# RWKV-6 followed by a SiLU feed-forward layer: four sums of weight slices moved to an earlier stage and another engine, one load moved to another buffer slot, a scaling moved to ScalarE

## The chip, the cores and the metric

The kernel runs on one core of a Trainium2 chip. The metric is the device time of one execution in microseconds (us); before the change it is 572.14 us, the median of 3 runs (571.52 to 572.37). Engines are called as in the profile: PE (TensorE), DVE (VectorE), ACT (ScalarE), POOL (GpSimd), SP (SyncE, which here only issues transfers).

## The reference

```python
# r, k, v, w: (4 batches, 8 heads, 768 tokens, 48), float32;  u: (8, 48)
for t in range(S):
    cur = u * k_t outer v_t
    y[:, :, t] = r_t @ (state + cur)
    state = w_t[:, None] * state + k_t outer v_t
x = y as (4 * 768 tokens, 8 * 48 = 384)
h = x @ w_in                 # 384 x 2048, given as float64
out = (h * sigmoid(h)) @ w_out   # 2048 x 384, given as float64
```

## The kernel before, in words

**Units.** The 768 tokens are cut into 6 stretches of 128, the 4 batches into 2 pairs. A unit is one stretch of one pair, so there are 12 units, numbered 0 to 11 here as in the code (the change's "fourth unit" is unit 3). Every unit passes three phases, and phases of different units run beside each other: attention of unit i, the first layer ("ups") of unit i-1, the second layer ("downs") of unit i-2.

**Attention of a unit.** r, k and w come in token order into `raw`, a buffer with two slots and rooms for w, r and k in each. Unit i uses slot i % 2 up to unit 3 and slot 0 from unit 4 on (`slot`, L98). DVE transposes the rooms into `tw`, `tr`, `tk` (`turn`, L361). The 128 x 128 score matrix is built in 7 levels: at each, POOL multiplies keys by products of decays (`start_keys` L666, `grow_own` L651, `grow_keys` L642; the products themselves are L410), DVE does so with the queries (`grow_queries` L624, `prepare` L779), PE multiplies them (L700), and the result is kept in `score` by DVE (`keep_masked`, L718) or ACT (`keep_level`, L800). Two levels go to PE together, in a "burst" at levels 1, 3 and 5. The diagonal, the bonus with u, is summed apart: up to unit 3 by `bonus` (POOL, L436 to L440), `bonus_sum` (DVE, L445 and L449, then four small transfers), `bonus_spread` (ACT copies L588 and L590, a DVE shuffle L591) and `bonus_write` (DVE, L598, one for each half e of the heads); from unit 4 on in blocks of 8 tokens by `block_bonus` (POOL, L493), `block_sum` (DVE, L530), transfers through DRAM, `block_turn` (L563) and `block_write` (L569). Then `y_state` (PE, L843 and L850) and `y_values` (PE L864, ACT copies L869) make y, and `update` makes the new state: PE products (L909), the old state scaled by the decay, and DVE's sum of both (L932). The scaling is done by POOL for units 2 and 3 (L914, two multiplications) and by ACT from unit 4 on (L927, eight activations of 48 columns).

**The weights** arrive as float64. Sixteen pieces (eight of w_in, eight of w_out) are rounded to float32 by ACT (L228, L230, L236), DVE (L247, L248) and POOL (L260), up to about 99 us.

**The feed-forward layers.** From unit 1 on the second layer is a product of 2 x 2 blocks done with seven multiplications (`quarter`, L1329; "quarter 6" is the last of them), on sums of activations (`sums`, DVE, L1300) and on four sums of w_out blocks (`weight_sums`, DVE, L1285). A quarter's result leaves PSUM by L1334 (ACT) or L1337 (DVE). From unit 3 on (`NFAST`) the first layer is done with 20 multiplications on sums of slices of x (`sums_of_x`, DVE) and of w_in (`in_weight_sum`, L1124): 21 additions of 128 x 512, named m, n, q14, q3 and so on in `weight_plan`. Their results stand in eight rooms: two in `in_sum`, six in slot 1 of `raw` (two each in its w, r and k rooms), or in place in `w_in_sb`. Their first reader is unit 3's first layer (L1185), which starts at 190.79 us in the profile.

**Order of the work.** Each engine runs its queue in the order in which the Python code issues it (no scheduler). The first three units are written out by hand in `do(...)` lists at the end; from unit 3 on `mix(i)` gives a list of groups, and after each group a number of steps of the downs and ups is issued. The loop that calls `mix` appends the weight sums to groups by number: six names for DVE (m in group 4, n in 5, m1 and m2 in 6, q12a and q12 in 8; `weight_sums(3)` second in group 4), the rest on POOL (q14 and q3 in group 7, q, n13 and t in 10, u1, u and q19 in 11; the last seven names, in the next unit, are left where they are).

Of the kernel before, what the change touches and what calls it, by code (L numbers as in the profile page):

```python
# [38 lines left out]
def kernel(  # L39
# [11 lines left out]
    nc = tc.nc  # L51
# [4 lines left out]
    NL = 7  # L56
    NB = 2
# [9 lines left out]
    NSLOT = 2  # L67
    NTOK = 2
    NPAIR = 4
# [28 lines left out]

    def slot(i, name):

        return 0 if i >= NPAIR else i % NSLOT

    def twos(room):

# [354 lines left out]
    at = 768  # L459
# [441 lines left out]
    def update(i, b):  # L901
        n, b0 = units[i]
        if n == S // L - 1:
            return
        if b == 0:
            p_kv[i] = bank("p_m" if i < NTOK else "p_sc", NB, NP, D)
        for p in range(NP):
            for e in range(2):
                nc.tensor.matmul(p_kv[i][PD * e:PD * e + D, b, p, :], lhsT=kq[i, b][:, p, PD * e:PD * e + D],  # L909
                                 rhs=values(i, b)[:, 2 * p + e, :], start=(b == 0 and p == 0),  # L910
                                 stop=(b == NB - 1 and p == NP - 1))
        new = state[:, b0 + b]
        if n > 0 and i < NPAIR:
            nc.gpsimd.tensor_tensor(out=new, in0=new,  # L914
                                    in1=tw[i][NL][:, b * NP:(b + 1) * NP, :].to_broadcast([128, NP, D]),
                                    op=ALU.mult)
        if b == NB - 1 and i < NPAIR:
            add_update(i)

    def add_update(i):  # L920
        n, b0 = units[i]
        if n == S // L - 1:
            return
        for b in range(NB if i >= NPAIR else 0):
# [30 lines left out]
    def both(fn, i, *args):  # L955
        return [(fn, i, b, *args) for b in range(NB)]
# [4 lines left out]
    def mix(i):  # L961

        ahead = i + 1 < len(units)

        def at(now, *steps):
            return steps if now else ()

        def bonus_steps(j, *steps):
            return [(block_bonus, j, x) for x in steps]

        def sum_steps(j, *steps):
            return [(block_sum, j, x) for x in steps]
# [7 lines left out]
        def products_of(j, *ls):  # L980
            return [(product, j, l) for l in ls]

        end = [[*at(ahead, *bonus_steps(i + 1, 0, 1, 2, 3))],
               [*at(i < len(units) - NB, (turn_apart, i), (turn_k, i)), (y_state, i), *both(y_values, i), *at(ahead, *turns(i + 1)), *at(ahead and i > NFAST, *sum_steps(i + 1, 0, 1)),
                *at(i <= NFAST, (sums, i - 1, FH // 2 - 2)), *both(update, i), *at(not ahead, (move_x, i))]]
        if i < NPAIR:
# [5 lines left out]
                      [(prepare, i, 3), (reverse_v, i), (bonus, i, 0), (bonus_sum, i, 0)],  # L992
                      [(bonus, i, 1), (burst, i, 3), (keep_level, i, 3), (bonus, i, 2)],
                      [(keep_level, i, 4), (go_on, i, 4), (bonus_sum, i, 1), (load_rk, i + 1), (load_u,)],
                      [(prepare, i, 5), (make_block_mask,), (bonus_spread, i)],
                      [(burst, i, 5), (keep_level, i, 5, 0), (keep_level, i, 6, 0), (go_on, i, 6), *at(i == NPAIR - 1, *both(turn, i + 1, "w")), (bonus_write, i, (0,)), (keep_level, i, 5, 1), (keep_level, i, 6, 1), (bonus_write, i, (1,))], *end]
            groups = list(zip(groups, (1, 1, 0, 2, 1, 1, 1, 1, 1, 2, 2, 1, 1)))
        else:
            j = i - 1
# [21 lines left out]
            else:  # L1021
# [3 lines left out]
                def loads(name, *gs):  # L1025
# [18 lines left out]
                          ([(burst, i, 5), (keep_level, i, 5, 0), (keep_level, i, 6, 0), *at(ahead, *bonus_steps(i + 1, 0)), (go_on, i, 6), (block_turn, i), *at(i > NPAIR + 1, (block_write, i, 1))], 2),  # L1044
# [319 lines left out]
    def do(*steps):  # L1364
        for fn, *args in steps:
            fn(*args)
# [39 lines left out]
    for m in range(1, 4):  # L1406
# [4 lines left out]
    do((scores, 1, NL - 1), (bonus, 2, 0), (bonus, 2, 1), (join_weight, 8), (add_weight,), (bonus_sum, 2, 0), (bonus, 2, 2), (up, 0, 7), (turn_apart, 1), *both(x_products, 1),  # L1411
       (turn_k, 1), *both(x_copy, 1), (tail_weight, 9), (head_weight, 9),
       (join_weight, 9), (add_weight,), *both(update, 1), (up, 1, 0), (tail_weight, 10), (head_weight, 10), (bonus_sum, 2, 1), *both(turn, 2, "w"))
# [22 lines left out]
    for i in range(3, len(units)):  # L1436
        steps = downs(i - 2) + ups(i - 1)
        groups = mix(i)
        if i == NTOK + 1:
            groups[4][0].insert(1, (weight_sums, 3))  # L1440
            for place, engine, names in ((4, nc.vector, ("m",)), (5, nc.vector, ("n",)), (6, nc.vector, ("m1", "m2")), (7, nc.gpsimd, ("q14", "q3")),
                                         (8, nc.vector, ("q12a", "q12")), (10, nc.gpsimd, ("q", "n13", "t")), (11, nc.gpsimd, ("u1", "u", "q19"))):
                groups[place][0].append((in_weight_sum, engine, *names))
        if i == NFAST + 1:
            keep_banks()
            for place, engine, names in ((5, nc.gpsimd, ("q7",)),
                                         (8, nc.gpsimd, ("q8", "q1")), (9, nc.gpsimd, ("q5", "q9")), (14, nc.gpsimd, ("q6", "q17"))):
# [40 lines left out]
```

## Time and profile before

| | |
|---|---|
| time, median of 3 runs | 572.14 us (571.52 to 572.37) |
| the profiled execution's own time | 571.82 us |
| its span (first to last instruction) | 570.0 us |
| PE busy / weight loads | 556.4 us / 517.9 us |
| DVE / POOL / ACT busy | 477.6 / 396.8 / 270.6 us |
| granted TensorE clock | 0.997 of full speed |

The page of the profile gives busy time by engine, then the queues and the chain of work that ended last. The view of waits lists, for each engine, what ended its idle time. The timeline gives runs of equal instructions in order of time: start, duration from the first to the end of the last, engine, line, operation, tile written and tiles read, shapes, count, and in brackets the idle time ahead and what ended it.

### The profile page before, as it was taken

The numbers are of one execution on the slowest core, as the hardware profiler recorded it, in microseconds if no ns is written. First come the engines' busy times: TensorE is split into PE (matmuls) and PEld (weight loads), VectorE is DVE, ScalarE is ACT, GpSimd is POOL, SyncE is SP. The second block draws the span as 40 slices with busy tenths as digits, with TensorE's granted clock in tenths as the row PEclk, the third lists the DMA queues.
The fourth block names the chain that finished last, engine by engine and source line by source line (L and its number), as shares of the span: only waits on it lengthen the run. The fifth ranks groups of instructions, "written<-read, shape, count | busy, mean of one in ns | idle before, by whom it ended". The sixth has DMA issues, their size and how long they took to land.

```text
span 570.0 us, 18875 instructions
## 1 busy us (share of the span) xinstructions
PE 556.4 (98%) x7782; PEld 517.9 (91%) x7782; DVE 477.6 (84%) x745; ACT 270.6 (47%) x604; POOL 396.8 (70%) x450
## 2 busy tenths in 40 slices
PE   8989999999998999899999999999999999999997
PEld 7768776698888999899999999999999999999997
DVE  7979798898999899879989989989989989882250
ACT  5779695442451373273274274274274272371330
POOL 6998868637999998795696696696696696700000
PEclk9989999999999999999999999999999999999999
DMA  9957776444255365265464465365465462102000
GB/s 224 316 114 204 183 230 113 49 84 101 74 90 100 69 112 94 58 130 93 73 129 89 87 120 94 71 128 94 93 106 96 91 109 65 37 6 56 29 9 21
DMA packets 206485, 57.59 MB, mean 101 GB/s; under 512 B 186048, under 2 KB 198208, under 8 KB 206400
## 3 DMA queue, kind: packets, MB, share of 16 engines
q1 hardware_dynamic: 203712, 54.23, 46.3%
q10 hardware_dynamic: 2688, 2.16, 1.6%
q8 instruction: 61, 1.00, 0.8%
q14 instruction: 24, 0.20, 0.1%
HBM read 47.14 MB, written 9.18 MB: 99 GB/s over the span
## 4 chain that ended last, share of the span: by engine, by line
PE 76%; DVE 9%; POOL 8%; issue 2%; DMA 2%; ACT 1%; SPq 1%; DVEq 0%; POOLq 0%
PE p_o L1329 24%; PE p_o L1185 15%; PE p_h L1185 10%; PE p_h L1078 6%; PE p_h L1329 4%; PE p_m L1267 4%; POOL tk L642 2%; PE p_sc L700 2%; PE p_m L864 2%; DVE temps L1300 2%; PE p_sc L1329 2%; DVE score L718 2%; PE p_m L843 1%; PE p_m L700 1%; DMA raw<-in_r_dram 1%
## 5 line engine op out<-in xcount | busy, mean ns | idle before, releaser
L642 POOL TENSOR_TENSOR tk<-tk,tw 128x256 f32<-128x256 f32 x112 | 93.2, 853 | 7.1 <-DVE tw L410 3.1
L1329 PE MATMUL p_o<-own,temps 128*128 128x192 f32 x496 | 82.9, 326 | 1.5 <-DVE temps L1300 1.5
L1329 PEld LDWEIGHTS p_o<-own,temps 128*128 128x128 f32 x496 | 80.8, 190 | 1.8 <-DVE temps L1300 1.8
L1185 PE MATMUL p_o<-xt,w_in_sb 128*64 128x128 f32 x1152 | 72.1, 273 | 0.6 <-POOL w_in_sb L1124 0.6
L1078 PE MATMUL p_h<-xt,w_in_sb 128*128 128x256 f32 x288 | 67.7, 391 | 0.8 <-POOL w_in_sb L260 0.8
L1185 PEld LDWEIGHTS p_o<-xt,w_in_sb 128*64 128x64 f32 x1152 | 64.7, 137 | 0.8 <-POOL w_in_sb L1124 0.8
L1078 PEld LDWEIGHTS p_h<-xt,w_in_sb 128*128 128x128 f32 x288 | 54.7, 194 | 9.4 <-POOL w_in_sb L260 1.1
L410 POOL TENSOR_TENSOR tw<-tw 128x256 f32<-128x256 f32 (+6 forms) x71 | 38.8, 546 | 33.0 <-DVE tw L361 29.6
L1329 PE MATMUL p_o<-w_out_sb,gt 128*128 128x192 f32 x308 | 54.4, 329 | 1.4 <-DVE ob L1337 1.4
L493 POOL TENSOR_TENSOR ruk<-tokens_rk 128x384 f32<-128x384 f32 x48 | 54.3, 1151 | 0.0
L1329 PEld LDWEIGHTS p_o<-w_out_sb,gt 128*128 128x128 f32 x308 | 50.1, 190 | 2.3 <-DVE ob L1337 1.7
L624 DVE TENSOR_TENSOR tr<-tr,tw 128x512 f32<-128x512 f32 x57 | 51.1, 896 | 0.6
L651 POOL TENSOR_TENSOR tk<-tk,tw 128x256 f32<-128x256 f32 x32 | 24.8, 806 | 30.7 <-DVE tk L361 30.7
L1300 DVE TENSOR_TENSOR temps<-gt 128x512 f32<-128x512 f32 (+1 forms) x48 | 44.6, 965 | 0.0
L1334 ACT COPY partial<-p_o 128x192 f32<-128x192 f32 x31 | 9.9, 319 | 70.5 <-PE p_o L1329 70.5
L612 ACT COPY tk<-tk 128x256 f32<-128x256 f32 x52 | 21.0, 403 | 38.0 <-POOL tk L642 29.0
L1209 ACT ACTIVATE gt<-p_o 128x512 f32<-128x512 f32 x45 | 26.1, 601 | 25.6 <-PE p_o L1185 25.6
L718 DVE COPY_PREDICATED score<-mask,p_sc 128x512 f32<-128x512 int8 x42 | 31.2, 798 | 0.8 <-PE p_sc L700 0.6
L1329 PE MATMUL p_o<-w_out_sb,temps 128*128 128x192 f32 x176 | 30.4, 326 | 0.0
L493 POOL TENSOR_TENSOR spare<-tokens_rk 128x384 f32<-128x384 f32 x24 | 29.1, 1228 | 0.6
L1329 PE MATMUL p_h<-w_out_sb,gt 128*128 128x192 f32 x168 | 29.1, 326 | 0.0
L1329 PEld LDWEIGHTS p_o<-w_out_sb,temps 128*128 128x128 f32 x176 | 28.9, 190 | 0.0
(252 smaller groups left out, 1308.0 us busy)
## 6 DMA issues: line engine op xcount, KB each, us to landing
w_out_sb<-in_moe_w_in_dram SPq DMA_DIRECT2D x6, 768.0 KB, 6.9
turned<-yt SPq DMA_DIRECT2D x18, 192.0 KB, 2.7
xt<-turned SPq DMA_DIRECT2D x9, 384.0 KB, 3.3
w_out_sb<-in_moe_w_out_dram SPq DMA_DIRECT2D x4, 768.0 KB, 5.1
own<-in_moe_w_out_dram SPq DMA_DIRECT2D x4, 768.0 KB, 6.5
tokens_w<-in_w_dram SPq DMA_DIRECT2D x8, 384.0 KB, 4.4
tokens_rk<-in_r_dram SPq DMA_DIRECT2D x7, 384.0 KB, 4.7
tokens_rk<-in_k_dram SPq DMA_DIRECT2D x7, 384.0 KB, 5.7
```

The source lines that it names most:

```text
L410: engine.tensor_tensor(out=up, in0=t[:, :, 0::2], in1=t[:, :, 1::2], op=ALU.mult)
L493: mul = lambda out, one, two: nc.gpsimd.tensor_tensor(out=out, in0=one, in1=two, op=ALU.mult)
L624: nc.vector.tensor_tensor(out=odd, in0=odd, in1=tw[i][l][:, :, 0::2][:, :, :, None].to_broadcast([128, Q, L >> (l + 1), c]), op=ALU.mult)
L642: nc.gpsimd.tensor_tensor(out=out, in0=have, in1=odd_products(i, l, b, *blocks), op=ALU.mult)
L651: nc.gpsimd.tensor_tensor(out=have, in0=have, in1=odd_products(i, l, b, [2, NP * ni]), op=ALU.mult)
L718: nc.vector.copy_predicated(out=dst, mask=masks[l][:, :, None].to_broadcast([128, NB, NP, ni, c]), data=sc[e].rearrange("p (b q) (i c) -> ...
L1078: nc.tensor.matmul(p_h[:, a, :], lhsT=w_in_sb[:, c, f * 128:(f + 1) * 128], rhs=xt[i][:, c, :], start=(a == 0 and c == 0), stop=(a == 1 an ...
L1185: nc.tensor.matmul(p[h:h + PD, q, :], lhsT=left[:, f:f + PD], rhs=right, start=first and q == 0, stop=q == 3, skip_group_check=True)
L1209: nc.scalar.activation(out=g(f, t), in_=have, func=AF.Silu)
L1267: nc.tensor.matmul(po[i, b], lhsT=gt[i, f // 2][:, f % 2, b * L:(b + 1) * L], rhs=w_out_sb[:, f, :], start=(f == 0), stop=(f == FC - 1))
L1300: nc.vector.tensor_tensor(out=out, in0=one, in1=two, op=op)
L1329: nc.tensor.matmul(p, lhsT=left(f), rhs=right[:, f, :], start=which in (0, 1, 3) and f == 0, stop=f == FH - 1, skip_group_check=True)
```

## The change

In words, by its parts:

- Unit 3's r is loaded into slot 0 of `raw` and not slot 1, so the r room of slot 1 is free from unit 1 on. The eight rooms are dealt out anew: m and t in `in_sum`, n and n13 in slot 1's w room, q14 and q3 in its r room, m1 and q12 in its k room.
- m, q14, q3 and q are summed on POOL in the hand-written list of the rounding: m and q14 behind `bonus(2, 2)`, q3 and q behind piece 9's addition. Before, m was DVE's and the others POOL's, all in unit 3.
- The other sums of unit 3: n goes from group 5 to 7, m1 and m2 from 6 to 8, q12a and q12 from 8 to 9 (all DVE), n13 and t from 10 to 9 (POOL). `weight_sums(3)` goes from the second to the last place of group 4.
- The state's scaling in units 2 and 3 goes from POOL (L914) to ACT (L927).
- Unit 3's `bonus_spread` goes from group 9 to 10, behind the first half's `keep_level`.
- In unit 5, `block_sum` 3 goes behind `keep_level(i, 3)`, and `block_write(i, 1)` goes two groups earlier, as in units 6 to 11.

```diff
     def slot(i, name):
-        return 0 if i >= NPAIR else i % NSLOT
+        return 0 if i >= NPAIR or (i, name) == (NPAIR - 1, "r") else i % NSLOT
...
-        if n > 0 and i < NPAIR:
+        if n > 0 and i < NTOK:
             nc.gpsimd.tensor_tensor(out=new, in0=new,
...
-        for b in range(NB if i >= NPAIR else 0):
+        for b in range(NB if i >= NTOK and n > 0 else 0):
...
-                      [(prepare, i, 5), (make_block_mask,), (bonus_spread, i)],
-                      [(burst, i, 5), ..., *both(turn, i + 1, "w")), (bonus_write, i, (0,)), ...
+                      [(prepare, i, 5), (make_block_mask,)],
+                      [(burst, i, 5), ..., *both(turn, i + 1, "w")), (bonus_spread, i), (bonus_write, i, (0,)), ...
...
-                          ([(burst, i, 3), *sum_steps(i, 3), (keep_level, i, 3), *sum_steps(i, 4)], 2),
+                          ([(burst, i, 3), *at(i > NPAIR + 1, *sum_steps(i, 3)), (keep_level, i, 3), *at(i == NPAIR + 1, *sum_steps(i, 3)), *sum_steps(i, 4)], 2),
...
-                          ([..., (block_turn, i), *at(i > NPAIR + 1, (block_write, i, 1))], 2),
+                          ([..., (block_turn, i), (block_write, i, 1)], 2),
                           ([(keep_level, i, 5, 1), (keep_level, i, 6, 1)], 1),
-                          ([*at(i == NPAIR + 1, (block_write, i, 1)), (block_write, i, 0)], 1),
+                          ([(block_write, i, 0)], 1),
...
-        e = dict(zip(("m", "n", "t", "n13", "m1", "q12", "q14", "q3"), rooms))
+        e = dict(zip(("m", "t", "n", "n13", "q14", "q3", "m1", "q12"), rooms))
...
-    do(..., (bonus, 2, 2), (up, 0, 7), ...
+    do(..., (bonus, 2, 2), (in_weight_sum, nc.gpsimd, "m", "q14"), (up, 0, 7), ...
-       (join_weight, 9), (add_weight,), *both(update, 1), ...
+       (join_weight, 9), (add_weight,), (in_weight_sum, nc.gpsimd, "q3", "q"), *both(update, 1), ...
...
-            groups[4][0].insert(1, (weight_sums, 3))
-            for place, engine, names in ((4, nc.vector, ("m",)), (5, nc.vector, ("n",)), (6, nc.vector, ("m1", "m2")), (7, nc.gpsimd, ("q14", "q3")),
-                                         (8, nc.vector, ("q12a", "q12")), (10, nc.gpsimd, ("q", "n13", "t")), (11, nc.gpsimd, ("u1", "u", "q19"))):
+            groups[4][0].append((weight_sums, 3))
+            for place, engine, names in ((7, nc.vector, ("n",)), (8, nc.vector, ("m1", "m2",)), (9, nc.vector, ("q12a", "q12",)), (9, nc.gpsimd, ("n13", "t",)), (11, nc.gpsimd, ("u1", "u", "q19",)),):
                 groups[place][0].append((in_weight_sum, engine, *names))
```

More of the change, by code (lines that the diff above doesn't have):

```diff
@@ L994, in mix @@
                       [(keep_level, i, 4), (go_on, i, 4), (bonus_sum, i, 1), (load_rk, i + 1), (load_u,)],
-                      [(prepare, i, 5), (make_block_mask,), (bonus_spread, i)],
-                      [(burst, i, 5), (keep_level, i, 5, 0), (keep_level, i, 6, 0), (go_on, i, 6), *at(i == NPAIR - 1, *both(turn, i + 1, "w")), (bonus_write, i, (0,)), (keep_level, i, 5, 1), (keep_level, i, 6, 1), (bonus_write, i, (1,))], *end]
+                      [(prepare, i, 5), (make_block_mask,)],
+                      [(burst, i, 5), (keep_level, i, 5, 0), (keep_level, i, 6, 0), (go_on, i, 6), *at(i == NPAIR - 1, *both(turn, i + 1, "w")), (bonus_spread, i), (bonus_write, i, (0,)), (keep_level, i, 5, 1), (keep_level, i, 6, 1), (bonus_write, i, (1,))], *end]
             groups = list(zip(groups, (1, 1, 0, 2, 1, 1, 1, 1, 1, 2, 2, 1, 1)))
@@ L1043, in mix @@
                           ([*loads("r", 3)], 1),
-                          ([(burst, i, 5), (keep_level, i, 5, 0), (keep_level, i, 6, 0), *at(ahead, *bonus_steps(i + 1, 0)), (go_on, i, 6), (block_turn, i), *at(i > NPAIR + 1, (block_write, i, 1))], 2),
+                          ([(burst, i, 5), (keep_level, i, 5, 0), (keep_level, i, 6, 0), *at(ahead, *bonus_steps(i + 1, 0)), (go_on, i, 6), (block_turn, i), (block_write, i, 1)], 2),
                           ([(keep_level, i, 5, 1), (keep_level, i, 6, 1)], 1),
-                          ([*at(i == NPAIR + 1, (block_write, i, 1)), (block_write, i, 0)], 1),
+                          ([(block_write, i, 0)], 1),
                           ([*at(ahead, *bonus_steps(i + 1, 1, 2, 3)), ], 2),
@@ L1409 @@
        (bonus_write, 1))
-    do((scores, 1, NL - 1), (bonus, 2, 0), (bonus, 2, 1), (join_weight, 8), (add_weight,), (bonus_sum, 2, 0), (bonus, 2, 2), (up, 0, 7), (turn_apart, 1), *both(x_products, 1),
+    do((scores, 1, NL - 1), (bonus, 2, 0), (bonus, 2, 1), (join_weight, 8), (add_weight,), (bonus_sum, 2, 0), (bonus, 2, 2), (in_weight_sum, nc.gpsimd, "m", "q14"), (up, 0, 7), (turn_apart, 1), *both(x_products, 1),
        (turn_k, 1), *both(x_copy, 1), (tail_weight, 9), (head_weight, 9),
-       (join_weight, 9), (add_weight,), *both(update, 1), (up, 1, 0), (tail_weight, 10), (head_weight, 10), (bonus_sum, 2, 1), *both(turn, 2, "w"))
+       (join_weight, 9), (add_weight,), (in_weight_sum, nc.gpsimd, "q3", "q"), *both(update, 1), (up, 1, 0), (tail_weight, 10), (head_weight, 10), (bonus_sum, 2, 1), *both(turn, 2, "w"))
     blocks = block_loads(3)
@@ L1445 @@
             keep_banks()
-            for place, engine, names in ((5, nc.gpsimd, ("q7",)),
-                                         (8, nc.gpsimd, ("q8", "q1")), (9, nc.gpsimd, ("q5", "q9")), (14, nc.gpsimd, ("q6", "q17"))):
+            for place, engine, names in ((5, nc.gpsimd, ("q7",)), (8, nc.gpsimd, ("q8", "q1",)), (9, nc.gpsimd, ("q5", "q9",)), (14, nc.gpsimd, ("q6", "q17",)),):
                 groups[place][0].append((in_weight_sum, engine, *names))
```

## The prediction, as put on record before the changed kernel ran

> **What bounds the kernel.** I read the busy shares first, then who PE waited for, then the timelines of PE, DVE and POOL around each of those waits. The first page gives (busy us, share, instructions):
>
> ```profile
> PE 556.4 (98%) x7782; PEld 517.9 (91%) x7782; DVE 477.6 (84%) x745; ACT 270.6 (47%) x604; POOL 396.8 (70%) x450
> ```
>
> PE is the bound. The change leaves PE's instructions as they are, so it can only give what PE idles. The waits (total us, times, longest) are few:
>
> ```profile
> PE p_sc L700 <- POOL tk L666: 1.5, 1, 1.5
> PE p_o L1329 <- DVE temps L1300: 1.5, 1, 1.5
> PE p_o L1329 <- DVE ob L1337: 1.4, 1, 1.4
> PE p_m L1372 <- POOL ident masks.py:199: 1.4, 1, 1.4
> PE p_m L700 <- POOL tk L642: 1.3, 2, 1.0
> PE p_m L850 <- DMA raw<-in_r_dram: 0.9, 1, 0.9
> ...
> PE p_o L1185 <- POOL w_in_sb L1124: 0.6, 1, 0.6
> ```
>
> PE's timeline places them. The first and the fourth lie ahead of 40 us, where nothing changes. Six lie in the changed stretch: 1.03 us at 133.56 (unit 3's first burst), 1.47 at 178.45, 0.56 at 202.05, 1.38 at 231.77, 0.23 at 249.33, 0.88 at 257.97. They add up to **5.55 us**, the most that can be won. After 258 us PE never waits, so what is won there stays won.
>
> Behind these waits two engines are full. The table by stretches (us, then PE, weight loads, DVE, ACT, POOL) shows DVE and POOL both over 92% busy:
>
> ```profile
> 135.00:178.50 43.50, 42.03 (x442) 38.15 (x440) 41.36 (x55) 14.94 (x38) 40.03 (x40) 1.00 0.46 90
> ```
>
> And they slow each other. The same DVE addition of 128 x 256 takes 0.41 us while POOL idles (103.06) and 1.22 us beside POOL; two equal POOL multiplications take 1.47 us together at 92.20, and 2.94 us at 130.57 beside a DVE subtraction of 1.74 us:
>
> ```profile
> 103.06 0.41 DVE L1300 TENSOR_TENSOR temps<-temps,gt 128x256 f32<-128x256 f32 x1
> 163.70 1.22 DVE L1300 TENSOR_TENSOR temps<-temps,gt 128x256 f32<-128x256 f32 x1
> 92.20 1.47 POOL L642 TENSOR_TENSOR tk<-tk,tw 128x256 f32<-128x256 f32 x2 [0.39 <-ACT tk L612]
> 130.57 2.94 POOL L642 TENSOR_TENSOR tk<-tk,tw 128x256 f32<-128x256 f32 x2 [0.57 <-ACT tk L612]
> 130.46 1.74 DVE L1285 TENSOR_TENSOR w_out_sb<-w_out_sb,own 128x1536 f32<-128x1536 f32 x1
> ```
>
> **Part by part.**
>
> *Four sums into the rounding.* POOL idles there twice:
>
> ```profile
> 73.10 1.83 POOL L260 TENSOR_TENSOR w_out_sb<-temps 128x768 uint32<-128x768 uint32 x1 [2.44 <-DMA raw<-in_r_dram]
> 78.36 1.82 POOL L260 TENSOR_TENSOR w_out_sb<-temps 128x768 uint32<-128x768 uint32 x1 [3.43 <-ACT temps L228]
> ```
>
> L1124 on POOL costs 1.27 us undisturbed (155.03; 193.84), two of them 2.55, in gaps of 2.44 and 3.43. DVE does roundings, PSUM copies and transposes meanwhile, which keep their length beside POOL (L247 0.96 at 71.01 with POOL idle, 0.93 at 79.37 beside L260). The first gap overflows by 0.1 us. The additions' reader is PE's second layer: piece 11's L260 ends at 83.65, and its blocks f = 6, 7 come in the later half of PE's L1267 group at 83.66, so about 1.3 us of slack. At the slowest L1124 on POOL (2.30 at 158.07) the four would take 9.2 us, 3.3 more than the gaps, and PE would lose 2.0. I take 0, since the undisturbed row fits. The sums read only w_in, rounded by 63 us, and slot 1's r room was last read for unit 1; unit 3's r goes to slot 0 at 104.9, after unit 2's r was transposed (81.28 to 82.6); unit 4's r is issued at 156.69, after unit 3's transpose at 127.4. So the moved load waits for nothing and stays in its place in SP's queue.
>
> What it removes later: on DVE m (0.73); on POOL q14 and q3 (2.95 at 147.02) and q (1.27).
>
> *Scaling on ACT.* Removed from POOL: 2.04 us at 118.97 and 1.34 at 173.26. Added to ACT: eight activations, 1.91 us at 217.64. In unit 2 they stand behind the copies of y (L869, 119.97 to 122.34), so they end at 124.25, and DVE's L932 starts at 124.3 and not 123.47: **+0.85 us** for DVE's queue, whose next are unit 3's transposes, for which POOL (L410, L666, L642) and then the burst at 133.56 wait. In unit 3 they end at 170.0, long before L932 (175.79), and push one L1087 and the issue of x_out by 0.15 us; sums_of_x reads that x only at 184.53, so nothing.
>
> *`weight_sums(3)` behind the masked copies.* The 1.74 us subtraction no longer stands beside L642: that pair goes from 2.94 to 1.47. With +0.85 the keys are ready at 133.56 + 0.85 - 1.47 = 132.95 against PE's 132.53: the wait falls from 1.03 to 0.4 (between 0 and 1.9, if nothing is relieved). The subtraction now ends about 137.0; quarter 6 reads its result at 139.49, or 138.9 with PE earlier: covered by 1.9.
>
> *Wait at 178.45.* DVE has hardly any idle time from 137 to 178, so its own gain decides. It loses m (0.73) and n's 1.48 goes to a place where DVE would wait for the burst at 142.18; `bonus_sum` then comes about 1 us earlier, and POOL, without q14 and q3, does level 4's keys at 147.1 and not 149.97. I put the end of `bonus_write` at 160.6, before it is 161.43: 0.85. It can't be much earlier, since ACT copies both_b 1.04 us later than before, behind the first four-and-two L800: at about 156.8, and the second L800 end at 158.6. Then come 16 sums (L1300). POOL's bonus of unit 4, held behind q, n13 and t until 160.32 so far, starts when its r and k have landed, about 156.4, and is through with u1, u, q19 and L410 at 169.4; the last of the first eight sums runs free, which gives 0.4 more. DVE's gain is 1.25; with a little for L914 gone, **1.5 us**, which is PE's whole gain up to here (0.6 at 133 is inside it). Bounds: 0, if POOL's removed work is filled by the work behind it; 2.1 (1.47 + 0.6), the whole wait.
>
> The Trainium skill, "SBUF — State Buffer", section "Who interferes with whom", states that a DVE instruction with two SBUF inputs and a GpSimd one that reads SBUF exclude each other for a whole instruction. The rows above agree (the pair is longer by 1.47 beside 1.74). If that were the entire account, the POOL work taken out before 178 in unit 3 (2.95 + 1.27 + 1.34) would come off DVE's queue whole and the wait would be gone, a sum better by 0.6. My sum stays with the queue as walked through.
>
> *Wait at 202.05* is for q9. POOL does q7, q8 and q1 before level 4's L642 (197.68), whose ACT copy is ready at 197.19. With POOL earlier, that copy, which follows PE, becomes the gate: 0.49 earlier. **0.5** (0 to 0.56).
>
> *Wait at 231.77.* DVE's queue stands 0.89 us behind POOL's L493, which follows the DVE transposes of unit 5, slowed by POOL before. Relative to PE, POOL is earlier by that same 0.5 only: **0.5** (0 to 1.38). At 249.33: 0.1 (0 to 0.23).
>
> *Unit 5's order.* The releaser named at 257.97 is a transfer long done; DVE's row shows the real one:
>
> ```profile
> 254.30 3.61 DVE L569 COPY_PREDICATED score<-spare 128x1024 f32<-128x1024 int8 x2 [0.72 <-ACT score L800]
> 257.81 2.09 DVE L1300 TENSOR_TENSOR temps<-gt 128x512 f32<-128x512 f32 x2
> ```
>
> The second of two L569 ends at 257.8. Now one runs at 251.1 (DVE is idle 1.77 us there, and block_both has landed, as the shuffle at 250.89 shows) and the other ends near 255.4, against PE's 257.09: **0.88** (0.5 to 0.88). `block_sum` 3 behind `keep_level` moves DVE's work between two waits for POOL: 0.
>
> **Sum:** 1.5 + 0.5 + 0.5 + 0.1 + 0.88 = 3.5 us off 571.82, the profiled execution (span 570.0 and 1.8 around it): 568.3. The median of the runs is 0.3 higher, so **568.6 us**.
>
> **Rivals.**
>
> - *All six waits go.* POOL's earlier sums free both queues enough. For it: both are over 92% full. Against it: after 195 us POOL's gates are ACT copies that follow PE. 572.14 - 5.55 = 566.6.
> - *DVE stays as late at 178.* The freed POOL time is filled at once by unit 4's bonus, which then disturbs the same DVE sums. Only 0.5 and 0.88 remain: 570.8.
> - *It doesn't do what it says:* PE's waits reappear at the next instruction, as its chain alternates between DVE and POOL. Against it: after 258 us nothing waits. 572.1.
> - *Slower: the late sums hold up DVE.* n, m1, m2, q12a and q12 now run beside level 4's and 5's L642 and n13, t; they took 6.2 us (0.68 to 2.18 each). At 2.18 each they take 10.9: 4.7 more, less 0.73 for m and 1.4 won elsewhere, is +2.6: 574.7. It decides from 9.5 us for the five. Against it: POOL has less to do there now.
>
> **Chances.** Forecast 0.50, all waits gone 0.14, DVE as late 0.13, nothing 0.12, slower 0.11. The case of 570.8 is split by the bound of 0.2% (1.14 us, about what a measurement here can tell from no change: below 571.0 is faster): 0.09 faster, 0.04 same. Faster 0.73, same 0.16, slower 0.11. The range takes in all waits gone and no change: 566.3 to 572.3.
>
> **What would show it.** Right: L1124 on POOL between 70 and 78 us with L260 at its old times; L642 after the first transposes of unit 3 at about 1.5 us a pair and PE's wait there under 0.6; the wait before L1329 near 177 under 0.7; L569's second end before PE's L850 in unit 5. Wrong: a new PE wait between 78 and 130 (rounding held up), L932 at 125 or later, or DVE's L1124 of over 1.9 us each.

## The result, and the profile after

The changed kernel takes **570.47 us** (median of 8 runs, 569.81 to 571.70), the kernel before in the same comparison 572.23 us (8 runs): a ratio of 0.9973, 95% interval 0.9962 to 0.9984. The gain is 1.76 us, half of the 3.5 forecast. The profiled execution was one of the slower ones of the changed kernel (571.49 us, span 569.7), and so was the one in a second profile of it, from run e1 below (571.38 us, where the median is 570.16), which stands beside it in what follows.

The first page of the changed kernel (busy us, share, instructions) and its view of waits for PE (total, times, longest):

```profile
PE 555.2 (97%) x7782; PEld 516.5 (91%) x7782; DVE 476.4 (84%) x744; ACT 274.6 (48%) x620; POOL 394.5 (69%) x447
```

```profile
PE p_o L1329 <- DVE temps L1300: 1.6, 1, 1.6
...
PE p_o L1329 <- DVE ob L1337: 1.2, 1, 1.2
PE p_m L1267 <- POOL w_out_sb L260: 0.9, 1, 0.9
...
PE p_m L700 <- POOL tk L642: 0.6, 2, 0.4
PE p_o L1185 <- POOL w_in_sb L1124: 0.3, 1, 0.3
```

The largest wait in the changed stretch, for DVE's L1300, has not shrunk. A new one has come (L1267, for a rounding). The one for POOL's L642 is down from 1.0 to 0.4, and that for L569 in unit 5 is gone.

PE does the same 7782 matmuls in the same order in both, so the time between two fixed PE instructions compares the kernels stretch by stretch, whatever came before. In us:

| from, to (start in the profile before) | before | after | e1 | e10 |
|---|---|---|---|---|
| rounding: L1267 (78.33) to L1267 (92.17) | 13.84 | 15.16 | 14.34 | 13.84 |
| unit 3's first burst, first product to second (133.56) | 1.73 | 1.06 | 1.06 | 1.06 |
| unit 3's L843 (163.52) to unit 4's third burst (189.70) | 26.18 | 26.31 | 26.45 | 24.57 |
| to unit 4's L843 (211.06) | 21.36 | 21.32 | 21.14 | 21.87 |
| to unit 5's third burst (234.56) | 23.50 | 23.29 | 23.48 | 22.86 |
| unit 5's L843 (255.96) to L909 (259.79) | 3.83 | 2.64 | 2.65 | 2.64 |

The other stretches of these profiles are alike to 0.3 us; the work before 66 us, which the change doesn't touch, ends between 0.2 us earlier and 0.9 us later than in the profile before (in e1 0.9, in e5 3.3).

**Rounding.** POOL's timeline (start, us from the first to the end of the last, instruction, count, and in brackets the idle time ahead) in the changed kernel:

```profile
67.59 0.99 POOL L436 TENSOR_TENSOR spare<-tokens_rk 128x384 f32<-128x384 f32 x1 [4.51 <-DMA tokens_rk<-in_k_dram]
...
75.11 1.29 POOL L1124 TENSOR_TENSOR raw<-w_in_sb 128x512 f32<-128x512 f32 x1
76.34 1.84 POOL L260 TENSOR_TENSOR w_out_sb<-temps 128x768 uint32<-128x768 uint32 x1
...
80.61 1.85 POOL L260 TENSOR_TENSOR w_out_sb<-temps 128x768 uint32<-128x768 uint32 x1
```

The four sums cost what was forecast, 1.3 us each. But unit 2's r and k landed 3.3 us later than in the profile before (L436 at 67.59, there 64.32), and with the gaps filled POOL can't catch up: L260 stands at 76.34 and 80.61, before at 73.10 and 78.36, and PE waits 0.92 us for it at 85.99.

**The sums of unit 3 (L1300), for which PE waits near 178 us.** DVE's timeline of the changed kernel, from the end of `bonus_write` on:

```profile
162.34 2.36 DVE L1300 TENSOR_TENSOR temps<-gt 128x256 f32<-128x256 f32 x2
164.62 1.23 DVE L1300 TENSOR_TENSOR temps<-temps,gt 128x256 f32<-128x256 f32 x1
165.89 1.38 DVE L1300 TENSOR_TENSOR temps<-gt,temps 128x256 f32<-128x256 f32 x1
167.19 2.91 DVE L1300 TENSOR_TENSOR temps<-gt 128x256 f32<-128x256 f32 x2
170.02 1.26 DVE L1300 TENSOR_TENSOR temps<-temps,gt 128x256 f32<-128x256 f32 x1
171.31 0.42 DVE L1300 TENSOR_TENSOR temps<-gt,temps 128x256 f32<-128x256 f32 x1
172.14 1.30 DVE L361 STREAM_TRANSPOSE tk<-raw 128x512 f32<-128x512 f32 x2 [0.40 <-DMA raw<-in_w_dram]
...
177.40 1.82 DVE L1300 TENSOR_TENSOR temps<-gt 128x256 f32<-128x256 f32 x2
179.15 0.41 DVE L1300 TENSOR_TENSOR temps<-temps,gt 128x256 f32<-128x256 f32 x1
```

and POOL's beside them:

```profile
159.29 3.97 POOL L493 TENSOR_TENSOR ruk<-ruk,u_bc 128x384 f32<-128x384 f32 x2
...
165.53 1.46 POOL L1124 TENSOR_TENSOR w_in_sb<-w_in_sb 128x512 f32<-128x512 f32 x1
167.06 1.33 POOL L1124 TENSOR_TENSOR w_in_sb<-raw,w_in_sb 128x512 f32<-128x512 f32 x1
168.48 1.34 POOL L1124 TENSOR_TENSOR w_in_sb<-w_in_sb 128x512 f32<-128x512 f32 x1
...
177.33 1.61 POOL L651 TENSOR_TENSOR tk<-tk,tw 128x256 f32<-128x256 f32 x2
```

POOL's bonus of unit 4 (L493) and u1, u, q19 (the three L1124) start 2.5 to 3 us earlier than before, and the first eight sums still stand beside them: they take 9.39 us to the end of the eighth (171.73), before 9.75. Late in the queue the second pair of L651 now falls beside the last four sums: the pair of sums at 177.40 takes 1.82, before it took 1.03. PE starts when the fifteenth sum ends, at 179.56. The rows of the profile before, DVE's and then POOL's:

```profile
169.80 1.38 DVE L1300 TENSOR_TENSOR temps<-gt,temps 128x256 f32<-128x256 f32 x1
...
176.94 1.03 DVE L1300 TENSOR_TENSOR temps<-gt 128x256 f32<-128x256 f32 x2
```

```profile
179.17 1.44 POOL L651 TENSOR_TENSOR tk<-tk,tw 128x256 f32<-128x256 f32 x2
```

### The profile page after: what moved, and what is told of

It is laid out like the page before. It is cut to its first block, busy times and chain, and to the rows that moved or that the text cites. A ratio compares the mean times of both kernels' runs of the same rounds, so it can differ in the third digit from the quotient of the medians.

```text
span 569.7 us, 18886 instructions
## 1 busy us (share of the span) xinstructions
PE 555.2 (97%) x7782; PEld 516.5 (91%) x7782; DVE 476.4 (84%) x744; ACT 274.6 (48%) x620; POOL 394.5 (69%) x447
## 4 chain that ended last, share of the span: by engine, by line
PE 70%; DVE 11%; POOL 8%; DMA 3%; ACT 3%; SPq 2%; issue 2%; DVEq 0%; POOLq 0%; ACTq 0%
PE p_o L1329 24%; PE p_o L1185 14%; PE p_h L1185 9%; PE p_h L1329 4%; PE p_m L1267 3%; PE p_h L1078 2%; PE p_sc L700 2%; PE p_m L864 2%; POOL tk L642 2%; DVE temps L1300 2%; PE p_sc L1329 2%; DVE score L718 2%; DMA raw<-in_k_dram 2%; PE p_m L843 1%; PE p_m L700 1%
## 5 line engine op out<-in xcount | busy, mean ns | idle before, releaser
L642 POOL TENSOR_TENSOR tk<-tk,tw 128x256 f32<-128x256 f32 x112 | 90.7, 830 | 7.5 <-DVE tw L410 3.2
L1329 PE MATMUL p_o<-own,temps 128*128 128x192 f32 x496 | 82.9, 326 | 1.6 <-DVE temps L1300 1.6
L1329 PEld LDWEIGHTS p_o<-own,temps 128*128 128x128 f32 x496 | 80.8, 190 | 2.0 <-DVE temps L1300 1.9
L410 POOL TENSOR_TENSOR tw<-tw 128x256 f32<-128x256 f32 (+6 forms) x71 | 40.0, 563 | 44.8 <-DVE tw L361 41.3
L1078 PE MATMUL p_h<-xt,w_in_sb 128*128 128x256 f32 x288 | 66.1, 384 | 1.7 <-POOL w_in_sb L260 1.5
L493 POOL TENSOR_TENSOR ruk<-tokens_rk 128x384 f32<-128x384 f32 x48 | 53.7, 1138 | 3.9 <-DVE block_sums L530 2.0
L1329 PE MATMUL p_o<-w_out_sb,gt 128*128 128x192 f32 x308 | 54.5, 330 | 1.2 <-DVE ob L1337 1.2
L1329 PEld LDWEIGHTS p_o<-w_out_sb,gt 128*128 128x128 f32 x308 | 50.0, 190 | 2.2 <-DVE ob L1337 1.5
L624 DVE TENSOR_TENSOR tr<-tr,tw 128x512 f32<-128x512 f32 x57 | 49.7, 873 | 0.6
L651 POOL TENSOR_TENSOR tk<-tk,tw 128x256 f32<-128x256 f32 x32 | 24.8, 804 | 30.7 <-DVE tk L361 30.7
L1300 DVE TENSOR_TENSOR temps<-gt 128x512 f32<-128x512 f32 (+1 forms) x48 | 45.9, 992 | 0.0
L1329 PE MATMUL p_o<-w_out_sb,temps 128*128 128x192 f32 x176 | 30.4, 326 | 0.0
L1329 PE MATMUL p_h<-w_out_sb,gt 128*128 128x192 f32 x168 | 29.1, 326 | 0.0
L493 POOL TENSOR_TENSOR spare<-tokens_rk 128x384 f32<-128x384 f32 x24 | 28.5, 1199 | 0.6
L1329 PEld LDWEIGHTS p_o<-w_out_sb,temps 128*128 128x128 f32 x176 | 28.9, 190 | 0.0
```

What stands on the lines that cost most here:

```text
L410: engine.tensor_tensor(out=up, in0=t[:, :, 0::2], in1=t[:, :, 1::2], op=ALU.mult)
L493: mul = lambda out, one, two: nc.gpsimd.tensor_tensor(out=out, in0=one, in1=two, op=ALU.mult)
L624: nc.vector.tensor_tensor(out=odd, in0=odd, in1=tw[i][l][:, :, 0::2][:, :, :, None].to_broadcast([128, Q, L >> (l + 1), c]), op=ALU.mult)
L642: nc.gpsimd.tensor_tensor(out=out, in0=have, in1=odd_products(i, l, b, *blocks), op=ALU.mult)
L651: nc.gpsimd.tensor_tensor(out=have, in0=have, in1=odd_products(i, l, b, [2, NP * ni]), op=ALU.mult)
L1078: nc.tensor.matmul(p_h[:, a, :], lhsT=w_in_sb[:, c, f * 128:(f + 1) * 128], rhs=xt[i][:, c, :], start=(a == 0 and c == 0), stop=(a == 1 an ...
```

## The experiments

The theory at the start: PE's wait at 178 stays because DVE's sums run beside POOL's work whatever was removed earlier, the rest is unit 5's order, and the rounding takes something back. The rivals: DVE's queue ahead of the sums is too long (late sums, `weight_sums`, L932's wait), or the early sums give nothing at all. Times are medians, each with its ratio to the kernel before in the same comparison.

**e1, the changed kernel again**

> The changed kernel once more, nothing edited. In its first profile PE waited 0.92 us at 85.99 for the rounding, and unit 2's r and k landed 3.3 us later than in the profile before (POOL's L436 at 67.59 against 64.32), in a stretch that the change does not touch. Theory A (the late landing is chance, the early sums fit): L436 near 64, no PE wait between 78 and 90 above 0.3 us, span near 568.7. Theory B (the early sums themselves hold up the rounding): L436 near 64 and still a PE wait of 0.5 us or more there. Both: the wait near 178 stays above 1.2 us, the one before L850 in unit 5 is gone; time about 1.7 us under the kernel before.

570.16 us, 0.997 (0.9959 to 0.9980). The gain repeats. L436 came at 66.69, so neither theory's condition (near 64) was met. The table shows nearly the same stretches but for the rounding, which loses 0.50 here (PE waits 0.51 at 87.64, for DVE's L624); the first profile lost 1.32 there and 0.27 more in the stretch behind it.

**e2, the early sums back in unit 3**

```diff
-(in_weight_sum, nc.gpsimd, "m", "q14"), ... (in_weight_sum, nc.gpsimd, "q3", "q"),
+(4, nc.vector, ("m",)), (7, nc.gpsimd, ("q14", "q3")), (9, nc.gpsimd, ("q", "n13", "t"))
```

> The four early sums go back into unit 3 (m on VectorE in group 4, q14 and q3 on GpSimd in group 7, q ahead of n13 in group 9); rooms, scaling on ScalarE, later sums and unit 5 as changed. Theory A (early sums cost nothing in the rounding but buy little, since VectorE's end at 178 hardly moved): within 0.5 us of the changed kernel, wait at 178 about 1.5 to 2.0. Theory B (they hold up the rounding by about 0.9): 0.5 to 1 us faster than the changed kernel. Rival (they are what frees GpSimd and VectorE, as the forecast had it): 1 to 2 us slower than the changed kernel, with the wait at 178 above 2.5 us.

575.05 us, 1.0049 (1.0036 to 1.0061), 4.9 slower than e1. The rounding stretch is back at 13.84, but the stretch with 178 takes 31.65 us, with two waits for L1300 (1.61 and 2.85). The waits are not all of it: in this profile the granted clock is 0.5 from 178.5 to 185.3 us, and 36 products of L1329 behind the second wait take 8.24 us, where the changed kernel takes 6.12. So without the early sums the rest of the change is slower than the kernel before, and of the 5.2 us that the stretch with 178 is longer than in e1, 2.7 are longer waits and 2.1 the clock that fell meanwhile.

**e3, both scalings back on GpSimd**

```diff
-        if n > 0 and i < NTOK:
+        if n > 0 and i < NPAIR:
-        for b in range(NB if i >= NTOK and n > 0 else 0):
+        for b in range(NB if i >= NPAIR else 0):
```

> The state's scaling of units 2 and 3 back on GpSimd, all else as changed. VectorE's L932 waited 1.37 us for ScalarE in the changed kernel. Theory A (that wait sits on the way to unit 3's first burst and to 178): L932 starts 1.3 us earlier relative to PE, the 0.36 us wait before the first burst goes, total 0.3 to 0.8 us faster than the changed kernel. Rival (the scaling in unit 3 on GpSimd, 1.3 us at about 173, disturbs VectorE's last sums): the wait at 178 grows by 0.5 to 1, total 0.3 to 0.8 slower.

570.29 us, 0.9966 (0.9957 to 0.9976). The wait before unit 3's first burst goes entirely (0.52 in that stretch and not 1.06), since L932 no longer waits for ACT. The wait at 178 is 1.78, beside 1.60 and 1.74 in the two profiles of the changed kernel, and from unit 3's first burst to unit 4's third PE is 0.41 to 0.55 us faster than in these two, so most of the 0.54 won at the burst is kept. The median doesn't show it (570.29 beside 570.16; the nine executions lie between 569.18 and 571.22).

**e4, unit 5's order alone on the kernel before**

> The kernel before with only unit 5's order changed (block_sum 3 behind keep_level 3, block_write of the second half two groups earlier). Theory A (that term was sized right): 0.9 us faster than before, the wait before L850 in unit 5 gone, all other PE waits as before. Rival (it only works together with an earlier GpSimd): under 0.4 us, or the wait moves to another place in unit 5.

570.77 us, 0.998 (0.9970 to 0.9989): 1.49 of the gain. In its trace every other wait is that of the kernel before (1.03, 1.50, 0.56, 1.39), and the stretch of unit 5 is 2.64. All the rest of the change is worth 0.6 us by these medians, and the single executions of the two kernels overlap (570.37 to 571.45, in e1 569.50 to 571.38), so even that is not certain.

**e5, DVE's late sums at their old groups**

```diff
-(7, nc.vector, ("n",)), (8, nc.vector, ("m1", "m2",)), (9, nc.vector, ("q12a", "q12",)),
+(5, nc.vector, ("n",)), (6, nc.vector, ("m1", "m2",)), (8, nc.vector, ("q12a", "q12",)),
```

> The changed kernel with VectorE's late sums at their old groups (n in 5, m1 and m2 in 6, q12a and q12 in 8); the four early sums stay early. In the changed kernel VectorE idles 2.4 us between 134 and 144 and does q12a and q12 (1.85 us) after 154.9. Theory C (VectorE's queue up to 178 sets the wait there, and putting its sums later gave the freed time away as idle time): the wait at 178 falls from 1.6 to under 0.4, 1.2 to 1.7 us faster than the changed kernel. Rival D (GpSimd's products beside the last L1300 set it, whatever stands earlier in VectorE's queue): the wait stays above 1.2, time as the changed kernel within 0.4.

570.60 us, 0.9978 (0.9969 to 0.9988), no difference from the changed kernel. The wait at 178 is 1.50. The rival was right.

**e6, q12a and q12 left out**

> The changed kernel without q12a and q12 at all: two of VectorE's additions (1.85 us at 154.9) are left out, so the products that read q12 take old data. Theory C: VectorE's end comes 1.4 to 1.9 us earlier, the wait at 178 goes to under 0.4, time 1.2 to 1.7 us under the changed kernel. Rival D: the L1300 only start earlier beside more of GpSimd's bonus work, the end moves by under 0.6, time within 0.6 of the changed kernel.

569.38 us, 0.9954 (0.9941 to 0.9967). With 1.85 us of DVE's work out ahead of the sums, the wait only falls to 1.15: DVE then idles 1.22 us for PE's burst 5 and 0.44 for ACT's `bonus_spread`. From there on DVE follows PE; a shorter queue ahead can't help much.

**e7, the early sums in POOL's gap after unit 2's last level**

```diff
-(in_weight_sum, nc.gpsimd, "m", "q14"), ... (in_weight_sum, nc.gpsimd, "q3", "q"),
+(load_values, 3), (in_weight_sum, nc.gpsimd, "m", "q14", "q3", "q"), (turn_apart, 2), ...
```

> The changed kernel with the four early sums not in the rounding but later, in GpSimd's idle gap of 17 us between unit 2's last keys (111.2) and unit 3's transposes (128.5). Theory B (in the rounding they hold up the second layer, PE lost 0.5 and 1.6 us between 78 and 117 in two profiles): that stretch is back at the 39.4 us of the kernel before, 0.5 to 1.5 us faster than the changed kernel. Rival: beside VectorE's sums and subtractions at 112 to 122 they slow VectorE, the state's sum and unit 3's first burst come 1 to 2 us later, and it is equal or slower.

571.26 us, 0.9984 (0.9975 to 0.9992), slower than the changed kernel. The rounding is back at 13.85, but POOL's four sums (110.66 to 116.16) now stand beside four of DVE's sums L1300, which take 1.27, 1.49, 1.48 and 1.38 us and not 0.42 each as in e1. DVE's masked copy L598 behind them keeps its length (2.48) and starts late, at 117.43; PE waits 0.43 for it at 119.96, and 0.83 at the burst.

**e8, `weight_sums(3)` in its old place**

```diff
-            groups[4][0].append((weight_sums, 3))
+            groups[4][0].insert(1, (weight_sums, 3))
```

> The changed kernel with weight_sums(3) back in second place of group 4, ahead of the masked copies. Forecast and theory C: the pair of L642 ahead of unit 3's first burst is back at about 2.9 us, PE's wait there 0.36 + 1.4 = 1.8 us, but part of it is given back at 178, where VectorE is late anyway: 0 to 0.9 slower than the changed kernel. Rival (the place does not matter): wait there under 0.6, time equal within 0.3.

573.00 us, 1.0011 (1.0000 to 1.0022): about 2.5 us slower than the changed kernel. The wait before the burst is 1.86 and not 0.36: with L932 late, the subtraction (131.97) stands right in front of the burst, and the pair of L642 beside it takes 2.95 and not 1.44. The next stretch, to burst 3, is 1.68 longer for another reason, the granted clock, which is 0.5 from 136.0 to 139.4 us in this profile; sixteen products there take 4.55 us, in the changed kernel 2.87:

```profile
135.69 4.55 PE L1329 MATMUL p_o<-own,temps 128*128 128x192 f32 x16
```

So the order itself is worth 1.5 us here; how many of the twelve executions had such a fall of the clock is not told.

**e9, u1, u and q19 left out**

> The changed kernel without u1, u and q19 at all: 3.95 us of GpSimd work at 165.5 to 169.8 is left out, so the products that read u and q19 take old data; VectorE's instructions are untouched. Leaving out 1.85 us of VectorE's queue before the third burst moved the wait at 178 by only 0.4, since VectorE then waits for that burst. Theory E (from that burst on VectorE has more to do than PE, because its sums run beside GpSimd's): the eight L1300 there get 2 to 3 us shorter together, the wait at 178 goes to under 0.3, time 1.2 to 2 us under the changed kernel. Rival F (VectorE is held by other things behind the burst, ScalarE's copies or the transposes, not by GpSimd): the L1300 keep their length to within 1 us, the wait stays above 1.0.

567.68 us, 0.9924 (0.9913 to 0.9936). The wait at 178 is gone, the first eight sums take 6.15 us and not 9.39, and the second four of the first eight sums take their undisturbed length (0.75 for two, 0.41, 0.42).

**e10, u1, u and q19 behind unit 4's second pair of L651; nothing is left out**

```diff
-(9, nc.gpsimd, ("n13", "t",)), (11, nc.gpsimd, ("u1", "u", "q19",)),):
+(9, nc.gpsimd, ("n13", "t",)),):
...
             keep_banks()
+            groups[1][0].insert(7, (in_weight_sum, nc.gpsimd, "u1", "u", "q19"))
```

> The changed kernel with u1, u and q19 moved behind unit 4's second pair of L651 (about 179), nothing left out. Theory E: the wait at 178 falls to under 0.5, but GpSimd's queue is 2 to 3 us later up to q9, so the wait at 203 grows from 0.34 to 1.5 to 2.5: total between 0.8 faster and 0.8 slower than the changed kernel. Rival F: the wait at 178 stays above 1.0 and the one at 203 grows, 1 to 2 us slower.

**568.69 us**, 0.9942 (0.9930 to 0.9954): faster than both kernels. DVE's timeline:

```profile
160.43 2.35 DVE L1300 TENSOR_TENSOR temps<-gt 128x256 f32<-128x256 f32 x2
162.70 1.23 DVE L1300 TENSOR_TENSOR temps<-temps,gt 128x256 f32<-128x256 f32 x1
163.97 1.15 DVE L1300 TENSOR_TENSOR temps<-gt,temps 128x256 f32<-128x256 f32 x1
165.04 0.75 DVE L1300 TENSOR_TENSOR temps<-gt 128x256 f32<-128x256 f32 x2
165.71 0.41 DVE L1300 TENSOR_TENSOR temps<-temps,gt 128x256 f32<-128x256 f32 x1
166.15 0.42 DVE L1300 TENSOR_TENSOR temps<-gt,temps 128x256 f32<-128x256 f32 x1
...
174.00 1.48 DVE L1300 TENSOR_TENSOR temps<-temps,gt 128x256 f32<-128x256 f32 x1
```

From the first sum to the end of the eighth it is 6.14 us, in the changed kernel 9.39. The three POOL sums now stand beside the last four (1.48 for one that took 0.41), but those begin 11.81 us after the first sum and not 15.06, and PE doesn't wait. The same sums, the same tiles: only what POOL does at that moment has changed. The Trainium skill, "SBUF — State Buffer", section "Who interferes with whom", says that a DVE instruction with two SBUF inputs and a GpSimd instruction that reads SBUF share a read port, one at a time; the rows agree, 0.41 beside an idle POOL and 1.2 to 1.5 beside its L493 and L1124.

**e11, unit 5's order and `weight_sums(3)` last, on the kernel before**

> The kernel before with two parts of the change alone: unit 5's order, and weight_sums(3) last in group 4. The early sums, the slots and the scaling are as before. From the trace so far: 1.3 us from unit 5 and the whole 1.03 us wait before unit 3's first burst, nothing lost in the rounding: 2.0 to 2.4 us under the kernel before, about 0.2 under the changed kernel. Rival (the early sums are needed to pass the gain on, VectorE being late at 178 without them): 1.3 to 1.5 us under the kernel before, the wait at 178 up by 0.7 to 1.

571.39 us, 0.9989 (0.9980 to 0.9998): slower than unit 5's order alone. The burst comes at once (0.52), but `weight_sums(3)` (1.78 us at 134.65) then pushes DVE's other work: the stretch to unit 3's L843 is 0.97 longer, and the wait at 178 is 1.88. The stretch with 178 takes 28.28, but 1.7 of that is the granted clock, 0.5 from 179.6 to 183.0 us, which fell after that wait in this profile; in seven of the eleven executions the mean clock was 1.000. Without the early sums the place of `weight_sums(3)` won nothing here.

**e12, unit 2's scaling on GpSimd, unit 3's on ACT**

> The changed kernel with unit 2's scaling of the state back on GpSimd and unit 3's on ScalarE. VectorE's 1.37 us wait at L932 goes and so does PE's 0.36 before unit 3's first burst (both did when both scalings were on GpSimd): 0.4 to 0.6 us faster than the changed kernel, the wait at 178 unchanged to within 0.3. Rival (the wait at 178 takes it back): equal within 0.2, the wait at 178 up by 0.5.

570.23 us, 0.9973 (0.9962 to 0.9984), as the changed kernel: no wait at the burst (0.52), 1.75 at 178. L932's wait for ACT is unit 2's. As in e3, PE is faster than in the changed kernel's two profiles up to unit 4's third burst (by 0.44 to 0.58), and the median doesn't show it.

**e13, e10 and e12 together**

> The changed kernel with u1, u and q19 later, and unit 2's scaling back on GpSimd (unit 3's stays on ScalarE), so that unit 3's first burst comes about 0.5 us earlier (1.06 to 0.52 in the stretch ahead of it, as unit 2's scaling on GpSimd gave alone). Theory (from burst 5 on DVE follows PE, and has room once u1, u and q19 are away): the 0.5 us carry through to the end, no wait returns before L1329 at 178: 568.2 us. Rival (DVE is full up to 178 for its own reasons): a wait of about 0.5 us appears at 178 instead, 568.7 us as without it.

569.00 us, 0.9945 (0.9933 to 0.9958), not faster than e10. In its profile r and k landed late again (POOL idle 4.53 before L436), and the rounding with the stretch behind it lost 1.65 us. In the later stretches, from the burst on, it is 0.4 us ahead of e10, most of what the burst wins, with no wait at 178. The theory fits the stretches; the median doesn't show it.

**e14, e10 with the early sums in POOL's gap**

> The changed kernel with u1, u and q19 later, and the four early sums in GpSimd's gap after unit 2's last level instead of beside the rounding. Theory: the rounding is never late (0.3 us on average, up to 1.6 in single executions), but unit 3's first burst is, by 0.7 before burst 3 of unit 2's end and 0.5 at the burst, as this place cost without u later: 569.3 to 569.7 us, slower than with u later alone (568.7). Rival: with DVE's queue relieved later on, that delay is absorbed: 568.4 us, the rounding's mean loss won.

569.28 us, 0.9952 (0.9938 to 0.9965), slower than e10. The rounding is at 13.85, and PE waits 0.41 for L598 and 0.83 at the burst, as in e7: that place costs the same with DVE relieved later.

**e15, u1, u and q19 later in the kernel before**

> The kernel before, with u1, u and q19 alone moved behind unit 4's second L651 pair. Theory (the wait before L1329 at 178 is these three instructions beside DVE's sums, in the kernel before as in the changed one): the wait of 1.5 us goes, and the waits at 202 and 231 stay at about 0.5 and 1.4: 570.6 us. Rival (in the kernel before, the queue ahead, with m, n, q14, q3 and q in unit 3, keeps DVE late anyway): at least 1 us of the wait stays, 571.6 to 572.1 us.

573.62 us, 1.0028 (1.0017 to 1.0040): the rival had the wait right, which stays (1.97), but neither had the time; it is slower. POOL's and DVE's timelines of this run, in one list each:

```profile
160.89 3.17 POOL L493 TENSOR_TENSOR ruk<-tokens_rk 128x384 f32<-128x384 f32 x2
...
167.59 1.07 POOL L493 TENSOR_TENSOR tokens_rk<-tokens_rk,tokens_w 128x384 f32<-128x384 f32 x1
...
177.75 1.44 POOL L1124 TENSOR_TENSOR w_in_sb<-w_in_sb 128x512 f32<-128x512 f32 x1
```

```profile
166.56 2.38 DVE L1300 TENSOR_TENSOR temps<-gt 128x256 f32<-128x256 f32 x2
...
177.99 1.48 DVE L1300 TENSOR_TENSOR temps<-temps,gt 128x256 f32<-128x256 f32 x1
```

In the kernel before, POOL's L493 doesn't begin until 160.9 and covers the first eight sums by itself up to 168.6; taking u1 to q19 away behind it relieves only the last two of the eight, and they then fall beside the last four, on which PE waits. So u1, u and q19 aren't the cause by themselves; it is what POOL's whole queue lays beside DVE's sums. Freeing the sums took both: u later, and the early sums, which bring L493 forward (it starts 2.1 to 2.3 us after unit 3's burst 5 in e10 and the changed kernel, 6.3 after it in the kernel before, e2 and e15). No run has these two parts alone.

## Why the prediction was half right

Its sign held, and its range; its sum of 3.5 was twice the gain. By its own steps (PE's stretches in the changed kernel and in e1, as gained against before; they add up to 0.5 and 1.5 us, where the medians differ by 1.76):

| step | forecast | after | e1 |
|---|---|---|---|
| four sums into the rounding | 0 | -1.6 | -0.5 |
| unit 3's first burst | 0.6 | 0.67 | 0.67 |
| the rest up to 178 | 0.9 | -0.13 | -0.27 |
| 202 | 0.5 | 0.04 | 0.22 |
| 231 | 0.5 | 0.21 | 0.02 |
| 249.33 | 0.1 | 0 | 0 |
| unit 5's order | 0.88 | 1.2 to 1.3 | 1.2 to 1.3 |

- **The step that failed is the wait at 178.45**, where the forecast took DVE's gain of 1.25 "with a little for L914 gone" to its end as 1.5 for PE; PE gained 0.54 up to there (0.40 in e1). Up to the eighth sum it was right: `bonus_write` ends at 162.34, which is 160.6 without what PE had lost by then (1.7), as forecast; the first eight sums gained 0.36, forecast 0.4. But the last eight were taken as unchanged. From the end of the eighth sum to the end of the fifteenth DVE takes 7.83 us, before 7.22: 0.40 idle before L361 and 0.79 for the pair at 177.40, less what others gained. POOL, with work taken off, now waits 1.93 us for DVE's L361 ahead of the first pair of L651, and from there its second pair reaches DVE's pair of sums as it starts; before, it came 2.2 us behind. In all 17 profiles the pair takes 1.82 or 1.83 us where the second L651 begins within 0.1 us of it (14), and 1.03 where it comes behind (before, e4, e11).
- **The rival "DVE stays as late at 178"**, with a chance of 0.13, had the kind of mechanism (POOL's later work moves up and fills the time) and the time, 570.8. It named unit 4's bonus; what moved beside the last eight was L651. That its time fits is in part luck, since it had neither the burst's 0.67 nor the rounding's loss. e9 and e10 show the other half: with POOL idle beside the second four of the first eight, the wait goes although the pair still takes 1.83. e15 shows the limit.
- **The rounding was no free place.** The durations were right; the slack was read from one execution. How late r and k land decides most of it. POOL's idle time ahead of unit 2's L436, and the loss in the rounding stretch: with the early sums 1.52 to 2.12 (e5, e6, e9, e10) none; 2.82, 2.84 and 3.31 (e3, e1, e8) 0.46, 0.50, 0.35; 2.99 (e12) none, so the order is not strict; 4.51 and 4.53 (after, e13) 1.32 and 1.36. Without them 3.11 (e2) and 4.49 (e15) none. The gaps that POOL had were what absorbed a late landing. The forecast named 3.3 us over the gaps and a loss of 2.0 as its bound, by slow sums; the sums kept 1.29 us, and what came late was the transfer. One of its signs of being wrong, a new wait of PE between 78 and 130, was there (0.92 at 85.99).
- **The burst** gave 0.67, as forecast. L932 comes at 126.02, which is 0.85 later than before without the 1.70 that PE had lost by then, exactly the forecast; its wait for ACT is 1.37 because DVE's sums ahead of it, no longer beside L914, also end earlier. The pair of L642 took 1.44, forecast 1.47. e8 and e12 show the two parts: 1.5 saved by `weight_sums`, 0.54 lost by the scaling on ACT.
- **202 and 231** were counted as POOL's lead carried on, 1.0 us together, and gave 0.25. POOL's lead ends at 178 as well, since its next step waits for DVE's `block_sum` (L530), which stands behind the sums. In the changed kernel (POOL):

```profile
180.96 1.96 POOL L493 TENSOR_TENSOR ruk<-tokens_rk 128x384 f32<-128x384 f32 x2 [2.02 <-DVE block_sums L530]
183.87 3.76 POOL L642 TENSOR_TENSOR tk<-tk,tw 128x256 f32<-128x256 f32 x4 [0.95 <-ACT tk L612]
```

  In the profile before, POOL passes here without a pause, so the 2 to 3 us that it was ahead are idled away, and level 4's L642 comes 0.93 later on the clock (198.61, before 197.68) with PE 1.16 later at unit 4's third burst. In e10 POOL waits only 0.27 here; the wait at 202 goes, that at 231 falls to 0.74.
- **Unit 5's order** had the right mechanism and was undersized: 1.19 in its own stretch and 0.13 to 0.15 ahead of it, and 1.49 in the medians when alone (e4). The view of waits names 0.88 of idle time; without the wait L850 also starts 0.22 before the modelled end of L843 (257.63 beside 257.85), and its products take 0.09 less.
- "All six waits go" would have been 566.6; e10, with 178 and 202 gone, gains 3.34. The slower rival did not come: the late sums of DVE took 4.4 us, before 6.2, and their place is indifferent to the time (e5). That a wait won reappears further on holds in e11 alone, between the burst and 178; in the changed kernel most of the burst's 0.67 stays won, in e3 and e12 most of a further 0.54.

What stays open: how often r and k land late, which sets the mean loss in the rounding, and whether e13 beats e10 where they land early. No run undoes the moved load or the later `bonus_spread` by itself; in the changed kernel's timeline DVE reaches the shuffle L591 (158.54) without idle time, in e6, with DVE earlier, after 0.44.

## What to carry to other kernels

Work taken off a full queue isn't a gain in time until what stands behind it has been placed: list, for the engine that the bound engine waits on, what its neighbour will be doing beside each of its instructions after the move, up to the last one. A gap in one profile may be what absorbs a late transfer; look at where it begins in several executions before filling it. Undoing parts one at a time can mislead when they need each other (the early sums, the place of `weight_sums`, u later): try a part alone on the old kernel too.

## What the runs showed of the hardware that was not expected

- The same loads of unit 2's r and k let POOL's L436 begin between 64.0 and 68.2 us in 17 profiles, with POOL idle 1.1 to 4.5 us for them; PE's work at that time is apart by 1.1 us at most, but for e5, whose start was 3.3 later than before.
- DVE was idle for 0.40 us ahead of L361 at 172.14, put down to a transfer. The same 0.40 stands in eight of the 17 profiles, 0.2 in e3 and e15, and none to speak of in before, e2, e4, e5, e6, e8 and e11. It shows when the sum ahead is short (0.42 or 0.43 in the eight, 0.61 in the two, over 1.1 in six of the seven others), but e6 had a short one and 0.05 of idle time. The cause is not settled.
- DVE's masked copy L598 (two of 128 x 1024), with a mask and data as operands, takes 2.50 us with POOL idle (114.20) and, in one piece, 3.3 to 3.85 beside POOL (near 158).
- PE's granted clock fell to 0.5 of full speed for 3.4 us after waits of 1.86 (e8) and 1.88 (e11), and for 6.8 us after one of 1.61 (e2). The fall began 0.9 to 1.3 us after the wait's end, and 3.4 us of it cost PE 1.7. It didn't come after the waits of 1.74 to 1.97 near 178 us in e1, e3, e12 and e15. Near 38 us (41 in e5) every profile has a wait of 1.5 to 1.6, and the clock fell after it in 8 of 17. So a wait can cost nearly its length once more, and its length alone doesn't tell whether it will; compare the granted clock of two profiles before reading their stretches.
